# Attention over a cache, one token: V of a head as one load of long runs, its products after both halves of K

## The chip, the cores and the metric

The kernel runs on one core of one Trainium2 chip. The metric is device microseconds of one execution; lower is better.

## The reference

One token (`x` of 512 numbers) goes through two branches that a gate mixes. Branch A is attention of 32 query heads over 8 key/value heads with 32,768 cached rows of 128 numbers each; branch B is a small gated FFN. All tensors are bf16.

```python
def reference(A_x, A_k_cache, A_v_cache, A_wq, A_wo, B_x, B_w_gate, B_w_up, B_w_down, gate_w):
    x = A_x                                               # 1 x 1 x 512
    g = sigmoid((x * gate_w).sum(-1))
    q = (x @ A_wq) as 32 heads of 128                     # wq 512 x 4096
    k, v = each of the 8 cached heads, for 4 query heads  # 8 x 32768 x 128 each
    p = softmax(q @ k.T * 128 ** -0.5)
    a = (p @ v) as 4096 numbers @ A_wo                    # wo 4096 x 512
    b = (silu(x @ B_w_gate) * (x @ B_w_up)) @ B_w_down    # 512 x 1792, 1792 x 512
    return g * a + (1 - g) * b
```

K and V of one cached head are 8.4 MB each, so the eight heads are 134 MB; the five weights add 14 MB. Everything is read once.

## The kernel before

**The stream.** All large loads are issued by SyncE (SP) on one queue, in the order of the list `stream` (lines 67 to 71): wq, K half 0 of head 0, the gate and up weights (`F1`), K half 1 of head 0, the down weights (`F2`); then for each head `g` from 1 on K half 0 of `g`, V half 0 of `g - 1`, K half 1 of `g`, V half 1 of `g - 1`; at the end V of head 7 and wo. A half of K or V is 16,384 rows, 4.194 MB. It is read as 128 runs of 32 KB, one for each partition (lines 294 to 296).

**The slots.** `ring` has five slots of 32 KB a partition. `place` (lines 73 to 78) gives every load its slot: K halves in slots 0 and 2, V halves in 1 and 3, wq in 1, F1 in 4, wo in 2, and the last V half in 0. F2 has a tile of its own, `wd_t`. A load whose slot had another load before it waits in SP until that one is released (`before`, `released`, lines 79 to 83 and 243 to 247): for wq by its products (`sem_pe_q`), for F1 by the FFN's (`sem_pe_h`), for a K half by its scores (`sem_k`, raised by the last group of them), for a V half by its products (`sem_pv`). SP takes its list in order, so a load that waits holds back all behind it. Slot 3 also holds scratch at first: `q_sb`, and the FFN's `sg`, `t1` and `tr`; so the first V half that goes there waits for `sem_tT`, the last step of the FFN's activation (lines 267, 268).

**TensorE.** For each K half, `emit_k` transposes 128 tiles through PSUM in 16 fills (line 404), VectorE copies each fill to SBUF (line 732), and TensorE forms the scores of four fills at a time (line 418). In the middle of it `emit_pt` transposes the probabilities of the head before (line 465), and VectorE copies them to `ET` (line 767). `emit_pv` multiplies a V half by `ET` (line 485). `emit_max` and VectorE form the maximum over both halves (lines 450, 454, 747, 755), and ScalarE then takes the exponentials `P` (line 621). V lags one head: in the pass of head `g` TensorE does K half 0 of `g`, V half 0 of `g - 1`, K half 1, V half 1, the maximum. In the pass of head 0 there is no V yet, and the FFN's products (`emit_ffn`, line 372) take the place of V half 0; they write the PSUM banks `ps_g` and `ps_u`, which are also those of the second half's scores and of the transposed `P`. ScalarE's sigmoid (line 613) and VectorE's `emit_t` (lines 713 to 719) follow it.

**The end.** The last V half comes in two pieces of 2 MB (`sem_ldv`); wo comes in five pieces (`WO_CUT`), each with a semaphore of its own, and its products (line 569) follow the pieces. ScalarE and VectorE write the result row.

Of the kernel before, what the change touches and what calls it, by code (L numbers as in the profile page):

```python
# [5 lines left out]
ACT = mybir.ActivationFunctionType  # L6
# [6 lines left out]
def bass_gated_mix__gqa_block_cached__swiglu_ffn__decode_kernel(  # L13
# [50 lines left out]
    assert NI * PB == 32 and sum(WO_CUT) == WOJ  # L64


    stream = [("wq",), ("K", 0, 0), ("F1",), ("K", 0, 1), ("F2",)]
    for g in range(1, G):
        for hf in range(2):
            stream += [("K", g, hf), ("V", g - 1, hf)]  # L70
    stream += [("V", G - 1, 0), ("V", G - 1, 1), ("wo",)]

    place = {("wq",): 1, ("F1",): 4, ("wo",): 2}
    for g in range(G):
        for hf in range(2):
            place["K", g, hf] = 2 * hf
            place["V", g, hf] = 2 * hf + 1
    place["V", G - 1, 1] = 0
    before = {}
    for i, e in enumerate(stream):  # L80
        for d in stream[:i]:
# [3 lines left out]
    with ExitStack() as es:  # L85
# [8 lines left out]
        sem_ldv = S_("s_ldv")  # L94
        sem_f2 = S_("s_f2")
        sem_ldo = [S_(f"s_ldo{i}") for i in range(len(WO_CUT))]
        sem_x = S_("s_x")
# [132 lines left out]
            "p (k e b d) -> p k e b d", k=HB, e=2, b=2  # L230
        )

        def kv_slot(entry):
            return slot_of(entry).rearrange("p (r d) -> p r d", r=RH)

        wq_v = slot_of(("wq",)).rearrange("p (c n) -> p c n", c=KC)
        f1 = slot_of(("F1",))
# [14 lines left out]
        with nc.Block("main") as block:  # L252
# [8 lines left out]
            @block.sync  # L261
            def _(sp):
                for i, e in enumerate(stream):
                    ld = sem_ld[place[e]] if e in place else sem_f2
                    if e in before:
                        sp.wait_ge(*released[before[e]])
                    elif e == ("V", 0, 1):
                        sp.wait_ge(sem_tT, 1)
                    if e[0] == "wq":
                        sp.dma_start(wq_v, A_wq.rearrange("(p c) n -> p c n", c=KC)).then_inc(  # L270
                            ld, 16
                        )
                    elif e[0] == "F1":
                        sp.dma_start(wg, B_w_gate.rearrange("(p c) f -> p c f", c=KC)).then_inc(
                            ld, 16
                        )
                        sp.dma_start(wu, B_w_up.rearrange("(p c) f -> p c f", c=KC)).then_inc(
                            ld, 16
                        )
                    elif e[0] == "F2":  # L280
                        sp.dma_start(wd, B_w_down.rearrange("(p j) n -> p j n", j=FC)).then_inc(
                            ld, 16
                        )
                    elif e[0] == "wo":
                        src = A_wo.rearrange("(p j) n -> p j n", j=WOJ)
                        j0 = 0
                        for c, n in enumerate(WO_CUT):
                            sp.dma_start(wo_v[:, j0 : j0 + n, :], src[:, j0 : j0 + n, :]).then_inc(  # L288
                                sem_ldo[c], 16
                            )  # L290
                            j0 += n
                    else:
                        kind, g, hf = e
                        src = (A_k_cache if kind == "K" else A_v_cache)[
                            0, g, hf * (S // 2) : (hf + 1) * (S // 2), :
                        ].rearrange("(p r) d -> p r d", r=RH)
                        dst = kv_slot(e)
                        if e == ("V", G - 1, 1):
                            sp.dma_start(dst[:, : RH // 2, :], src[:, : RH // 2, :]).then_inc(
                                ld, 16  # L300
                            )
                            sp.dma_start(dst[:, RH // 2 :, :], src[:, RH // 2 :, :]).then_inc(
                                sem_ldv, 16
                            )
                        else:
                            sp.dma_start(dst, src).then_inc(ld, 16)
                sp.wait_ge(sem_res, 2)
                sp.dma_start(
                    out[0, :, :], row[0:1, :]
                ).then_inc(sem_out, 16)  # L310
                sp.wait_ge(sem_out, 16)

            @block.tensor
            def _(pe):
# [112 lines left out]
                    ins.then_inc(sem_sc, 1)  # L427

                def emit_k(hf):
                    e = ("K", 0, hf)  # L430
                    take(load_sem(e), 16)
                    done = 0
                    for q in range(FPH):
                        emit_fill(kv_slot(e), q)
                        if q + 1 >= NCG * (done + 1) + 2:
                            emit_scores(hf, done)
                            done += 1
                        if q == NCG and hf == 0:
                            emit_o()
                        if q == FPH // 2:  # L440
                            emit_pt(hf)
                    while done < NI:
                        emit_scores(hf, done)
                        done += 1
                    pe.sem_inc(sem_cp, -FPH)
# [23 lines left out]
                        )  # L469
                    ins.then_inc(sem_pt, 1)  # L470

                def emit_pv(hf, halves=False):
                    e = ("V", G - 1 if halves else 0, hf)
                    take(load_sem(e), 16)
                    pe.wait_ge(sem_ptc, hf + 1)
                    src = kv_slot(e).rearrange("p (i c t) d -> p i c t d", i=NI, c=NCG)
                    for i0 in range(0, NI, 2):
                        if i0 > 0 and halves:
                            emit_outb()
                            warm(7)  # L480
                            pe.wait_ge(sem_ldv, 16)
# [12 lines left out]
                    ins.then_inc(sem_pv, 1)  # L494
# [43 lines left out]
                pe.wait_ge(sem_ptc, 1)  # L538
                emit_pt(1)
                emit_o()  # L540
                emit_pv(0)
                pe.wait_ge(sem_em, 1)
                pe.matmul(
                    ps_e[:, 0:H],
# [35 lines left out]
            def _(act):  # L580
# [28 lines left out]
                    ).then_inc(sem_oc, 1)  # L609

                emit_oc(1)
                act.wait_ge(sem_pe_h, 1)
                act.activation(sg[:, :], ps_g, ACT.Sigmoid).then_inc(sem_sg, 1)
                for g in range(G):
                    act.wait_ge(sem_nbias, g + 1)
                    if g < G - 1:
# [1 line left out]
                    for hf in range(2):  # L618
                        f = 2 * g + hf
                        act.wait_ge(sem_pt, f + 1)  # L620
                        act.activation(  # L621
                            P[:, hf, :],
                            ps_sc[hf],
                            ACT.Exp,
                            bias=nbias[:, 0:1],
                            scale=SCALE,
                            accum_out=esum[:, g, hf : hf + 1],
                        ).then_inc(sem_exp, 1)
# [5 lines left out]
            def _(dve):  # L634
# [140 lines left out]
                with dve.Fori(0, G) as it:  # L775
                    for hf in range(2):
# [76 lines left out]
```

## Time and profile before

| what | value |
|---|---|
| time, median of 3 runs | 352.45 us (352.36 to 352.77) |
| the profiled execution's own time | 352.42 us |
| its span in the profile | 350.6 us |
| granted TensorE clock, mean | 0.912 |
| TensorE busy | 259.2 us, 74% |
| VectorE busy | 200.1 us, 57% |
| ScalarE busy | 19.9 us, 6% |
| load queue of SP | 6050 packets, 148.12 MB, 98.5% of 16 engines' span |
| K loads, issue to landing, median of 16 | 25.1 us |
| V loads of 4 MB, issue to landing, median of 15 | 32.8 us |
| wq load, issue to landing | 12.3 us |

The span runs from the first to the last instruction; some 1.8 us of the device time lie around it. Busy shares are of the span. A load's time from issue to landing holds its wait in the queue: SP issues a load as soon as its slot is free, and the DMA engines take the loads in order. In the order of time a row has the start and the duration in us, the engine, the line, the operation, what it writes and reads, the number of instructions merged into the row, and in brackets how long the engine had been idle and what ended that.

### The profile page before, as it was taken

The numbers are of one execution on the slowest core, as the hardware profiler recorded it, in microseconds if no ns is written. First come the engines' busy times: TensorE is split into PE (matmuls) and PEld (weight loads), VectorE is DVE, ScalarE is ACT, GpSimd is POOL, SyncE is SP. The second block draws the span as 40 slices with busy tenths as digits, with TensorE's granted clock in tenths as the row PEclk, the third lists the DMA queues.
The fourth block names the chain that finished last, engine by engine and source line by source line (L and its number), as shares of the span: only waits on it lengthen the run. The fifth ranks groups of instructions, "written<-read, shape, count | busy, mean of one in ns | idle before, by whom it ended". The sixth has DMA issues, their size and how long they took to land. (4 is left out here: it accounts for less than half of the span.)

```text
span 350.6 us, 5679 instructions
## 1 busy us (share of the span) xinstructions
PE 259.2 (74%) x2423; PEld 179.1 (51%) x2423; DVE 200.1 (57%) x368; ACT 19.9 (6%) x57; POOL 1.4 (0%) x8
## 2 busy tenths in 40 slices
PE   0449876989495886858595978858597939777686
PEld 0147153856282846546382847546474718454342
DVE  4148287779284675838283765748265926666210
ACT  1100000300100002000100001000100010000100
POOL 1000000000000000000000000000000000000000
PEclk9999999899989698989789698989769987999899
DMA  8999999999999999999999999999999999999995
GB/s 337 441 402 434 422 440 426 443 441 422 422 437 441 430 422 426 445 441 422 422 434 445 430 422 426 441 441 422 426 422 452 434 422 426 437 445 422 413 419 207
DMA packets 6060, 148.20 MB, mean 423 GB/s; under 512 B 675, under 2 KB 678, under 8 KB 1062
## 3 DMA queue, kind: packets, MB, share of 16 engines
q1 hardware_dynamic: 6050, 148.12, 98.5%
q8 instruction: 4, 0.07, 0.1%
q14 instruction: 2, 0.02, 0.0%
q10 hardware_dynamic: 4, 0.00, 0.0%
HBM read 148.11 MB, written 0.00 MB: 422 GB/s over the span
## 5 line engine op out<-in xcount | busy, mean ns | idle before, releaser
L732 DVE COPY ktT<-ps 128x1024 bf16<-128x1024 bf16 x256 | 163.1, 684 | 81.8 <-PE ps L404 79.2
L404 PE MATMUL ps<-ident_f,ring 128*128 128x128 f32 x1024 | 157.9, 310 | 48.0 <-PEq L317 48.0
L404 PEld LDWEIGHTS ps<-ident_f,ring 128*128 128x128 f32 x1024 | 132.9, 161 | 80.5 <-issue 57.1
L418 PE MATMUL ps<-ktT,qc 128*32 128x512 bf16 x512 | 41.6, 401 | 15.2 <-DVE ktT L732 15.1
L485 PE MATMUL ps<-ring,ET 128*16 128x512 bf16 x512 | 32.0, 393 | 2.8 <-PEq L317 2.1
L485 PEld LDWEIGHTS ps<-ring,ET 128*16 128x16 bf16 x512 | 12.5, 91 | 19.1 <-issue 7.6
L418 PEld LDWEIGHTS ps<-ktT,qc 128*32 128x32 bf16 x512 | 7.9, 95 | 28.0 <-DVE ktT L732 24.2
L737 DVE TENSOR_REDUCE pmaxf<-ps 128x1 f32<-128x512 f32 x16 | 11.1, 691 | 13.8 <-DVEq L736 13.8
L589 ACT ACTIVATE qc<-qz 128x112 bf16<-128x112 bf16 x8 | 2.4, 296 | 197.7 <-DVE gsel L755 194.2
L502 PEld LDWEIGHTS ps<-osel,pv_sb 128*128 128x128 f32 x80 | 11.9, 228 | 1.4 <-DVE pv_sb L773 1.0
L621 ACT ACTIVATE P<-ps,nbias 128x512 bf16<-128x512 f32 x16 | 10.8, 676 | 29.0 <-DVE gsel L755 29.0
L502 PE MATMUL ps<-osel,pv_sb 128*128 128x4 f32 x80 | 11.3, 265 | 0.8 <-DVE pv_sb L773 0.5
L773 DVE COPY pv_sb<-ps 128x512 f32<-128x512 f32 x10 | 6.8, 682 | 6.5 <-PE ps L485 6.5
L465 PE MATMUL ps<-ident,P 128*128 128x128 bf16 x72 | 7.0, 219 | 1.7 <-ACT P L621 1.2
L767 DVE COPY ET<-ps 128x512 bf16<-128x512 bf16 x18 | 7.5, 414 | 1.3 <-PE ps L465 1.3
L372 PE MATMUL ps<-ring,xT 128*1 128x448 bf16 x32 | 6.6, 984 | 0.0
L747 DVE TENSOR_REDUCE gm<-ps 1x4 f32<-1x128 f32 x8 | 2.2, 279 | 7.7 <-DVEq L746 7.7
L465 PEld LDWEIGHTS ps<-ident,P 128*128 128x128 bf16 x72 | 5.4, 98 | 2.1 <-ACT P L621 1.3
L345 PE MATMUL ps<-ring,xT 128*1 128x512 bf16 x32 | 3.6, 626 | 3.6 <-PEq L317 3.6
L454 PE MATMUL ps<-gm,ones_f 1*128 1x4 f32 x16 | 2.8, 243 | 4.6 <-PEq L317 4.6
L326 PE MATMUL ps<-ones_bf,x_row 1*128 1x1 bf16 x4 | 0.3, 173 | 7.9 <-DMA gw_row<-in_gate_w_dram 7.9
L692 DVE CAST ring<-ps 128x512 bf16<-128x512 f32 x2 | 1.3, 685 | 7.5 <-PE ps L345 7.5
(70 smaller groups left out, 50.3 us busy)
## 6 DMA issues: line engine op xcount, KB each, us to landing
ring<-in_A_k_cache_dram SPq DMA_DIRECT2D x16, 4096.0 KB, 25.1
ring<-in_A_v_cache_dram SPq DMA_DIRECT2D x15, 4096.0 KB, 32.8
ring<-in_A_wq_dram SPq DMA_DIRECT2D x1, 4096.0 KB, 12.3
ring<-in_A_v_cache_dram SPq DMA_DIRECT2D x2, 2048.0 KB, 29.4
ring<-in_A_wo_dram SPq DMA_DIRECT2D x1, 2048.0 KB, 22.4
ring<-in_B_w_gate_dram SPq DMA_DIRECT2D x1, 1792.0 KB, 25.3
ring<-in_B_w_up_dram SPq DMA_DIRECT2D x1, 1792.0 KB, 29.2
wd_t<-in_B_w_down_dram SPq DMA_DIRECT2D x1, 1792.0 KB, 43.3
```

The lines of the kernel that those rows point to most:

```text
L345: ins = pe.matmul(ps_q[i][32 * c : 32 * c + 1, :], xT[:, k : k + 1], wq_v[:, k, n0 : n0 + 512], start=(k == 0), stop=(k == KC - 1),)
L372: ins = pe.matmul(acc[32 * c : 32 * c + 1, :], xT[:, k : k + 1], wt[:, k, c * FW : (c + 1) * FW].rearrange("d (i j) -> d j i", j=FC), star ...
L404: ins = pe.transpose(stb[:, t * 64 : (t + 2) * 64], two.bitcast(FP32), ident_f[:, :])
L418: ins = pe.matmul(ps_sc[hf][32 * c : 32 * c + 32, :], qc[:, e, 24 - PB * i : 56 - PB * i], kt[:, e, :], start=(i == 0 and e == 0), stop=(i ...
L465: ins = pe.transpose(ps_pt[:, hf * 512 + m * 128 : hf * 512 + (m + 1) * 128], P[:, hf, m * 128 : (m + 1) * 128], ident[:, :],)
L485: ins = pe.matmul(ps_pv[32 * c : 32 * c + 2 * PB, :], ET[:, hf, col : col + 2 * PB], src[:, i0 : i0 + 2, c, 2 * m : 2 * m + 2, :].rearrang ...
L502: ins = pe.matmul(ps_m[:, M_OT : M_OT + HPG], pv_sb[:, r * DH : (r + 1) * DH], osel[:, r * HPG : (r + 1) * HPG], start=(r == 0), stop=(r = ...
L621: act.activation(P[:, hf, :], ps_sc[hf], ACT.Exp, bias=nbias[:, 0:1], scale=SCALE, accum_out=esum[:, g, hf : hf + 1],).then_inc(sem_exp, 1)
L732: dve.tensor_copy(ktT[:, q % NKT, :], pst[q % NST]).then_inc(sem_cp, 1)
L737: ins = dve.tensor_reduce(pmaxf[:, hf : hf + 1], ps_sc[hf], AX.X, ALU.max)
L767: dve.tensor_copy(ET[:, hf, :], ps_pt[:, hf * 512 : (hf + 1) * 512]).then_inc(sem_ptc, 1)
L773: dve.tensor_copy(pv_sb[:, :], ps_pv).then_inc(sem_pvc, 1)
```

## The change

V of a head becomes one load of 8.4 MB in which each partition gets one run of 64 KB; it fills slots 2 and 3. So that the rows of a partition stay the same ones for K and V, a K half now takes 32 KB out of each 64 KB. K halves are in slots 0 and 1. The stream is K half 0, K half 1, V of the head before. wq has slot 4, F1 has slot 2, and wo takes slot 4, where wq was. The last V goes to slots 0 and 1, where the last K was, as three loads (4 MB, 2 MB, 2 MB), the second after the release of K half 1.

TensorE does both K halves, then the maximum, then both products of V of the head before. In the pass of head 0 the FFN comes after the maximum and waits for both exponentials, since its banks are in use until then. ScalarE's sigmoid of the FFN follows the exponentials of head 0, and VectorE's `emit_t` follows the maximum of head 0. The load of V of head 0 waits for the FFN's products (F1's slot) and for `sem_tT` (the scratch in slot 3). All other arithmetic is the same.

```diff
-    stream = [("wq",), ("K", 0, 0), ("F1",), ("K", 0, 1), ("F2",)]
+    stream = [("wq",), ("K", 0, 0), ("K", 0, 1), ("F1",), ("F2",)]
     for g in range(1, G):
-        for hf in range(2):
-            stream += [("K", g, hf), ("V", g - 1, hf)]
-    stream += [("V", G - 1, 0), ("V", G - 1, 1), ("wo",)]
-
-    place = {("wq",): 1, ("F1",): 4, ("wo",): 2}
+        stream += [("K", g, 0), ("K", g, 1), ("V", g - 1)]
+    stream += [("V", G - 1), ("wo",)]
+    place = {("wq",): 4, ("F1",): 2, ("wo",): 4}
     for g in range(G):
-        for hf in range(2):
-            place["K", g, hf] = 2 * hf
-            place["V", g, hf] = 2 * hf + 1
-    place["V", G - 1, 1] = 0
+        place["K", g, 0] = 0
+        place["K", g, 1] = 1
+        place["V", g] = 2 if g < G - 1 else 0
...
+        def v_slot(s0):
+            return ring[:, s0 : s0 + 2, :].rearrange("p s (r d) -> p (s r) d", r=RH)
...
-                released[("V", g, hf)] = (sem_pv, 2 * g + hf + 3)
+            released[("V", g)] = (sem_pv, 2 * g + 4)
...
-                    elif e == ("V", 0, 1):
+                    if e == ("V", 0):
                         sp.wait_ge(sem_tT, 1)
...
+                    elif e[0] == "K":
+                        src = A_k_cache[0, e[1], :, :].rearrange("(p h r) d -> h p r d", h=2, r=RH)
+                        sp.dma_start(k_slot(e[2]), src[e[2]]).then_inc(ld, 16)
                     else:
...
+                        src = A_v_cache[0, e[1], :, :].rearrange("(p r) d -> p r d", r=2 * RH)
+                        if e[1] < G - 1:
+                            sp.dma_start(v_slot(2), src).then_inc(ld, 16)
+                            continue
+
+                        v = v_slot(0)
+                        r0 = 0
+                        for sem, n in (
+                            (sem_ldv[0], RH),
+                            (sem_ldv[1], RH // 2),
+                            (sem_ldv[2], RH // 2),
+                        ):
+                            if r0 == RH:
+                                sp.wait_ge(*released["K", G - 1, 1])
+                            sp.dma_start(v[:, r0 : r0 + n, :], src[:, r0 : r0 + n, :]).then_inc(
+                                sem, 16
...
                 with pe.Fori(0, G) as g:
                     emit_k(0)
+                    emit_k(1)
+                    emit_max()
                     with pe.If(g > 0):
                         emit_pv(0)
+                        emit_pv(1)
                     with pe.Else():
+                        pe.wait_ge(sem_exp, 4)
+                        pe.wait_ge(sem_ptc, 2)
                         emit_ffn()
                         pe.wait_ge(sem_t1, 2)
-                    emit_k(1)
-                    with pe.If(g > 0):
-                        emit_pv(1)
-                    emit_max()
...
                 emit_oc(1)
-                act.wait_ge(sem_pe_h, 1)
-                act.activation(sg[:, :], ps_g, ACT.Sigmoid).then_inc(sem_sg, 1)
                 for g in range(G):
...
                         ).then_inc(sem_exp, 1)
+                    if g == 0:
+                        act.wait_ge(sem_pe_h, 1)
+                        act.activation(sg[:, :], ps_g, ACT.Sigmoid).then_inc(sem_sg, 1)
                     emit_oc(g + 2)
...
-                        if hf == 0:
-                            with dve.If(it == 0):
-                                emit_t()
+                    with dve.If(it == 0):
+                        emit_t()
```

More of the change, by code (lines that the diff above doesn't have):

```diff
@@ L93, in bass_gated_mix__gqa_block_cached__swiglu_ffn__decode_kernel @@
         sem_ld = [S_(f"s_ld{i}") for i in range(NSLOT)]
-        sem_ldv = S_("s_ldv")
+        sem_ldv = [S_(f"s_ldv{i}") for i in range(3)]
         sem_f2 = S_("s_f2")
@@ L231, in bass_gated_mix__gqa_block_cached__swiglu_ffn__decode_kernel, with k_slot @@
         )
-        def kv_slot(entry):
-            return slot_of(entry).rearrange("p (r d) -> p r d", r=RH)
+        def k_slot(hf):
+            return ring[:, hf, :].rearrange("p (r d) -> p r d", r=RH)
+        def v_slot(s0):
+            return ring[:, s0 : s0 + 2, :].rearrange("p s (r d) -> p (s r) d", r=RH)
         wq_v = slot_of(("wq",)).rearrange("p (c n) -> p c n", c=KC)
@@ L291, in _ @@
                             j0 += n
-                    else:
[L293 to L300, printed above, removed]
-                            )
[L302 to L306, printed above, removed]
+                    elif e[0] == "K":
+                        src = A_k_cache[0, e[1], :, :].rearrange("(p h r) d -> h p r d", h=2, r=RH)
+                        sp.dma_start(k_slot(e[2]), src[e[2]]).then_inc(ld, 16)
+                    else:
+                        src = A_v_cache[0, e[1], :, :].rearrange("(p r) d -> p r d", r=2 * RH)
[13 more added lines that the diff above has]
+                                sem, 16
+                            )
+                            r0 += n
                 sp.wait_ge(sem_res, 2)
@@ L429, in emit_k @@
                 def emit_k(hf):
-                    e = ("K", 0, hf)
-                    take(load_sem(e), 16)
+                    take(load_sem(("K", 0, hf)), 16)
                     done = 0
                     for q in range(FPH):
-                        emit_fill(kv_slot(e), q)
+                        emit_fill(k_slot(hf), q)
                         if q + 1 >= NCG * (done + 1) + 2:
@@ L470, in emit_pt, with emit_pv @@
                     ins.then_inc(sem_pt, 1)
-                def emit_pv(hf, halves=False):
-                    e = ("V", G - 1 if halves else 0, hf)
-                    take(load_sem(e), 16)
+                def emit_pv(hf, halves=None):
+                    if halves is not None:
+                        pe.wait_ge(sem_ldv[hf], 16)
+                    elif hf == 0:
+                        take(load_sem(("V", 0)), 16)
                     pe.wait_ge(sem_ptc, hf + 1)
-                    src = kv_slot(e).rearrange("p (i c t) d -> p i c t d", i=NI, c=NCG)
+                    src = v_slot(0 if halves is not None else 2)[:, hf * RH : (hf + 1) * RH, :].rearrange(
+                        "p (i c t) d -> p i c t d", i=NI, c=NCG
+                    )
                     for i0 in range(0, NI, 2):
@@ L480, in emit_pv @@
                             warm(7)
-                            pe.wait_ge(sem_ldv, 16)
+                            pe.wait_ge(sem_ldv[2], 16)
                         for m in range(NM):
@@ L540, in _ @@
                 emit_o()
-                emit_pv(0)
+                emit_pv(0, halves=False)
                 pe.wait_ge(sem_em, 1)
```

## The prediction

> **What bounds the kernel now.** I read the page first, then the issues of the load queue, then the chain, then the order of time around the first head. On the page, the row of the DMA engines and the table of queues:
>
> ```profile
> DMA  8999999999999999999999999999999999999995
> ...
> q1 hardware_dynamic: 6050, 148.12, 98.5%
> ...
> DMA ring<-in_A_wo_dram 7%; PE ps L404 2%; PE ps L418 1%; SPq L288 0%; DVE ktT L732 0%; DVE row L824 0%; PE ps L569 0%; PE ps L465 0%
> ```
>
> All 38 inner slices have the 16 DMA engines at 9 tenths or more, the one load queue fills 98.5% of the span, and what ends last is the last load, wo. TensorE is busy for 74%, VectorE for 57%. So the kernel is one stream of 148 MB, and its time changes only if the stream stops, or if its bytes move at another rate. The chain's few percent of TensorE ahead of wo is only the release that let wo be issued at 320.8 us; wo then landed 25.6 us later because V stood in the queue ahead of it.
>
> The rate comes from the order of time: TensorE's first fill of a head waits for K half 0 from head 2 on.
>
> ```profile
> 95.44 3.87 PE L404 MATMUL ps<-ident_f,ring 128*128 128x128 f32 x20 [3.66 <-PEq L317]
> ...
> 289.74 4.49 PE L404 MATMUL ps<-ident_f,ring 128*128 128x128 f32 x20 [4.72 <-PEq L317]
> ```
>
> Heads 2 and 7 start 194.30 us apart, 38.86 us a head. A head is four loads of 4.194 MB, so 431.7 GB/s and **9.72 us a slot**. The same view gives the due times of the stream, which I need below: K half 0 of head 2 lands at 95.4, so the load ahead of it ends at 95.4 - 9.7 = 85.7.
>
> The queue never ran dry. Its issues around the first heads, in order of time:
>
> ```profile
> 37.22 0.33 SPq L306 DMA_DIRECT2D ring<-in_A_k_cache_dram  x1
> 37.59 0.43 SPq L306 DMA_DIRECT2D ring<-in_A_v_cache_dram  x1
> 58.16 0.33 SPq L306 DMA_DIRECT2D ring<-in_A_k_cache_dram  x1
> 58.53 0.43 SPq L306 DMA_DIRECT2D ring<-in_A_v_cache_dram  x1
> 75.17 0.33 SPq L306 DMA_DIRECT2D ring<-in_A_k_cache_dram  x1
> ```
>
> At 37.6 two slots are queued behind the FFN weights; the next is asked for at 58.2. K half 0 of head 2, issued at 75.2, lands 20 us later: the stream has some 8 us in hand there, and more elsewhere.
>
> **What the Trainium skill says.** "DMA: Bandwidth & Descriptors", section "Where 436 GB/s comes from": the write ports give 435.2 GB/s in all. The trace agrees with 431.7 as a rate close under it, so long runs can gain 0.8% of it at most. The same page, "Latency and other measured facts": a row pitch of 512 KiB in HBM read at 207 GB/s against 214 in full, and only megabyte pitches halved it. No run here has a pitch over 32 KB. "TensorE: Matmul & The Clock Gate", "Part 1: The HAM clock gate": after an idle window of about 3.4 us the array runs at half rate. The trace agrees: TensorE did little from 58.4 to 61.6 us, and the windows read 0.50 after it. "ScalarE: Activation LUTs", "What ACT_TABLE_LOAD costs": 1283 ns for a change of set; the trace has 1.28 us.
>
> **The change, part by part.**
>
> *Long runs.* V of heads 0 to 6 is 128 packets of 64 KB where it was 256 of 32 KB; the last V keeps 32 KB and 16 KB runs. That removes 7 x 128 = 896 packets, 56 on each of 16 engines. A packet's fixed cost: 32 packets of 32 KB an engine take 38.86 us, 1214 ns each; at 435.2/16 = 27.2 GB/s the bytes alone take 1205, so 9.7 ns at most. The trace's packet records say the same: a 32 KB packet takes 1218 ns and a 16 KB one 615, which leaves 12. Gain 56 x 12 = **0.67 us**; 0 if a run of 64 KB is cut in two.
>
> *Pitch.* A K half now reads 32 KB of every 64 KB, and V starts at each 64 KB. Bytes are the same. I take 0; bounds 0 (nothing here can rise above the port rate) and +1% of the 305 us of K and V, +3 us.
>
> *Order in the steady state.* A head, counted from the landing of its K half 0: half 0 takes TensorE 13.6 us (95.44 to about 109.0), half 1 then 11.9 (77.03 to 88.92), the maximum 2.5 to 3, so it is ready at 28. Half 1 landed at 9.7, V of the head before lands at 29.2, and its products take 2 x 1.9 us warm or 2 x 3.4 cold: done by 36, before K of the next head at 38.9. Releases against the queue: K half 0 freed at 13.3, needed by 29; half 1 freed at 25.3, needed by 39; V freed at 36, needed by 48.6. **Cost nothing**, covered by at least 12 us of queued loads; without that cover each microsecond late would be a microsecond of end. Moving emit_max ahead of the products costs nothing either: it fills the wait for V.
>
> *The tail.* The last V goes to slots 0 and 1, freed by K at about 13 and 25 us of a head and needed at 29 and 39. wo has a slot that has been free since the start. Bytes and pieces after the last K are as before and wo still ends last, so 0. The products of the second half come after the first whole half landed, at 328.5 as before.
>
> *The first head.* Here the order does reach the stream. The FFN now runs after K half 1 and the exponentials (its banks are those of the scores and the transposed P), V of head 0 takes the slot of the gate and up weights, and its load waits for the FFN and for tT. SP is one queue: the loads behind V (both K halves of head 2) wait with it. The lines that time it:
>
> ```profile
> 36.79 0.63 PE L418 MATMUL ps<-ktT,qc 128*32 128x512 bf16 x8 [0.94 <-DVE ktT L732]
> ...
> 37.39 6.64 PE L372 MATMUL ps<-ring,xT 128*1 128x448 bf16 x32
> ...
> 46.02 0.65 DVE L719 STREAM_TRANSPOSE tT<-ring 128x448 bf16<-128x448 bf16 x1
> ```
>
> ```profile
> 57.73 0.63 PE L418 MATMUL ps<-ktT,qc 128*32 128x512 bf16 x8 [0.94 <-DVE ktT L732]
> ...
> 61.44 1.28 ACT L621 ACT_TABLE_LOAD   x1
> ...
> 63.98 0.20 ACT L621 ACTIVATION_READ_ACCUMULATOR P<-ps,nbias 128x1 f32 x1
> ...
> 77.03 3.29 PE L404 MATMUL ps<-ident_f,ring 128*128 128x128 f32 x24
> ```
>
> Half 0 ends at 37.4. Half 1 (landed by then) takes 11.9 and some 0.2 for the reduce of half 0 that now stands in front of VectorE's first copy: 49.5. From the end of half 1 to the second exponential is 64.2 - 58.4 = 5.8: 55.3. The FFN starts at 55.5 and takes 6.64 warm: 62.1. From its end to the end of tT is 46.67 - 44.03 = 2.64: 64.8, and V is issued at **64.9**. TensorE has done little from 49.5 on, so part of the FFN runs at half clock: 0 to 1.7 us more (half of one 3.4 us window); I take 0.9: **65.8**. The sigmoid now lies between two exponentials, so two more table loads: one lies beside the FFN (at line 584 the load ran at 1.54 us, long before its wait ended), the other in head 1, where nobody waits for P before V lands. If the first stands behind the wait, +1.28.
>
> When is V due? In the stream V of head 0 covers the two places that end at 85.7. An empty queue needs the 12.3 us of the wq load from issue to landing, then 9.7 for the second 4 MB: 22.0. So the issue is due at 85.7 - 22.0 = **63.7**. V is 65.8 - 63.7 = **2.1 us late**, and all that follows is as much later. The wq row may hold a slow start of the very first load, so 0.7 less is possible. Packets of instruction fetch each delay one engine by about 1.1 us; some may now fall after the stop: 0 to +1.1.
>
> What is late next: half 0 of head 1 runs from 64.9 to about 78.8, half 1 to 90.7, and the two K loads of head 2 go out at 79 and 91 where 86 and 95 would do. Products of head 0 end by 99 at the latest; V of head 1 is needed by 105. So one stop, not a row of them.
>
> **Sum:** +2.1 - 0.67 = +1.4 us on this execution's own 352.42 (span 350.6 and 1.8 around it), 0.03 under the median shown: **353.8**.
>
> **The rivals.** *No stop* (0.27): a warm FFN, a short exponential chain or a quick start of an idle queue puts V in at its due time. Then only packets count: 352.42 - 0.67 = 351.8, same or just faster. For it: 64.9 warm is only 1.2 us past 63.7, and 0.7 of that may be the first load's own. Against: three of my four open terms make V later. It decides at an issue of 63.7. *A long stop* (0.13): a full window at half clock and the table load in line, 64.9 + 1.7 + 1.3 = 67.9, 4.2 late, 356.0. *The pitch costs* (0.12): 1% gives 353.8 + 3 = 356.9; the port rate, not HBM, binds in the trace, which speaks against it. *The runs are cut* in two packets of 32 KB: then the 0.67 is missing, 354.5; inside the likeliest case (0.48).
>
> **How the numbers follow.** A measurement of this kernel tells about 0.2%, 0.7 us, from no change: faster is under 351.75, slower over 353.15. No stop splits 0.10 faster, 0.17 same; the likeliest case 0.42 slower, 0.06 same; long stop 0.13 slower; pitch 0.11 slower, 0.01 same. That is 0.10, 0.24, 0.66. The likeliest case alone spans 352.9 to 354.9; with the others, 351.6 to 356.9.
>
> **What would show it.** Right: the issue of V of head 0 at 65 to 67 us, one slice near 65 us with a dip in GB/s, K of head 2 starting at 97 to 98, and 38.8 us a head after it. The FFN row over 6.64 us shows the half clock. Wrong: no dip (no stop), a period over 39 us a head (pitch), a second dip in any later slice (a release that I put as early), or packets not down by about 900.

## The result and the profile after

The changed kernel takes 354.04 us (median of 6 runs, 353.54 to 354.38) against 352.36 us for the kernel before beside it (352.22 to 352.77): a ratio of 1.0046, 95% interval 1.0033 to 1.0058. It is **slower by 1.7 us**; 353.8 was predicted. The profiled execution took 354.20 us with a span of 352.4, 1.8 more than the span of before. A ratio leaves out single runs that lie over 1.5% above the fastest of the same kernel; where there were such runs, their times are given.

The page of the changed kernel, its DMA rows and its load queue:

```profile
DMA  8999999898998999999999999989999899899995
GB/s 346 428 417 421 429 438 450 322 476 357 443 502 365 476 409 424 476 409 420 420 417 476 417 417 431 506 372 417 435 458 476 357 454 491 365 476 405 396 423 206
...
q1 hardware_dynamic: 5042, 148.11, 98.0%
```

1008 packets fewer (896 data packets, the rest completion writes of loads that no longer exist), the same bytes, and 98.0% of the span where it was 98.5%. A digit of 8 or a low GB/s alone is no stop: the profile books a packet whole where it starts, and the packets of V are twice as long, so slices swing more. The stop is found with narrow windows. The last three columns are the granted clock of TensorE, the DMA share and GB/s; the first two rows are for the FFN, the others for the stop:

```profile
56.00:57.00 1.00, 1.00 (x8) 0.12 (x4) 0.00 (x0) 0.59 (x1) 0.00 (x0) 0.50 1.14 492
58.00:59.00 1.00, 1.00 (x12) 0.13 (x4) 0.00 (x0) 0.00 (x0) 0.00 (x0) 0.61 0.91 393
...
62.00:63.00 1.00, 0.07 (x4) 0.00 (x0) 0.31 (x1) 0.54 (x1) 0.00 (x0) 1.00 1.06 459
63.00:64.00 1.00, 0.00 (x0) 0.00 (x0) 0.96 (x2) 0.00 (x0) 0.00 (x0) 1.00 0.31 131
64.00:65.00 1.00, 0.00 (x0) 0.00 (x0) 0.67 (x2) 0.00 (x0) 0.00 (x0) 1.00 0.15 66
65.00:66.00 1.00, 0.51 (x3) 0.54 (x4) 0.00 (x0) 0.00 (x0) 0.00 (x0) 0.81 2.45 803
```

From 63 to 65 us hardly a packet starts; then those of V start together. By the packet records an engine was idle for 1.7 us on the mean, and its first packet of V took 2.7 to 3.4 us where 2.42 is usual, another 0.75 us an engine. The cause is in the order of time of the changed kernel, the queue's issues and the FFN that they wait for:

```profile
37.31 12.29 SPq L295 DMA_DIRECT2D ring<-in_A_k_cache_dram  x2
...
55.31 1.28 ACT L641 ACT_TABLE_LOAD   x1
...
55.44 6.64 PE L380 MATMUL ps<-ring,xT 128*1 128x448 bf16 x32 [3.56 <-PEq L325]
...
64.06 0.65 DVE L732 STREAM_TRANSPOSE tT<-ring 128x448 bf16<-128x448 bf16 x1
64.80 0.33 SPq L299 DMA_DIRECT2D ring<-in_A_v_cache_dram  x1
```

In the kernel before the FFN takes the same 6.64 us, from 37.39 us, where the granted clock is 1.00:

```profile
40.00:42.00 2.00, 2.00 (x12) 0.26 (x8) 0.00 (x0) 0.00 (x0) 0.00 (x0) 1.00 1.03 429
```

V of head 0 is issued at 64.80 us, right after tT. A load lands engine by engine. By the trace's landing records the last engine finishes V at 86.75 us; in the kernel before the load in that place finished at 85.59. From there the stream runs without a stop, and faster than before:

```profile
135.32 2.67 PE L412 MATMUL ps<-ident_f,ring 128*128 128x128 f32 x20 [2.75 <-PEq L325]
...
290.44 4.04 PE L412 MATMUL ps<-ident_f,ring 128*128 128x128 f32 x20 [4.46 <-PEq L325]
```

Heads 3 and 7 start 155.12 us apart: 38.78 us a head against 38.86. What the prediction had put at nothing is the end. First the kernel before, then the changed one: the products of the last piece of V, and of the last piece of wo.

```profile
338.29 1.04 PE L485 MATMUL ps<-ring,ET 128*16 128x512 bf16 x16 [0.74 <-DMA ring<-in_A_v_cache_dram]
...
348.21 0.38 PE L569 MATMUL ps<-ring,O 128*1 128x256 bf16 x4 [0.24 <-DMA ring<-in_A_wo_dram]
```

```profile
338.97 1.04 PE L496 MATMUL ps<-ring,ET 128*16 128x512 bf16 x16 [0.83 <-DMA ring<-in_A_v_cache_dram]
...
350.01 0.38 PE L581 MATMUL ps<-ring,O 128*1 128x256 bf16 x4 [0.25 <-DMA ring<-in_A_wo_dram]
```

The changed kernel is only 0.68 us behind at the last V, and 1.80 behind at the last wo: the same 4 MB took 9.92 us before and 11.04 after. So the sum as measured is +1.16 (stop) - 0.48 (long runs) + 1.12 (end) = +1.80 us, the difference of the spans. The middle term is what is left between V of head 0 and the last V; six loads at 0.08 us a head give the same.

These are landings of the last engine. The mean of the 16 engines tells it otherwise: V of head 0 is 2.15 us late (84.20 before, 86.35 after), the last piece of V 1.72, the last piece of wo 1.74. So no further time was lost at the end. The stop cost the mean engine 2.15 us; the last engine showed only 1.16 of it at V, because the engines landed 2.0 us apart before and 0.7 us apart after, and the rest came to light at wo, where one engine had fallen behind again.

### The profile page after: what moved, and what is told of

Read it like the earlier page. It is cut to its first block, busy times and chain, and to the rows that moved or that the text cites. A ratio compares the mean times of both kernels' runs of the same rounds, so it can differ in the third digit from the quotient of the medians.

```text
span 352.4 us, 5661 instructions
## 1 busy us (share of the span) xinstructions
PE 266.1 (76%) x2423; PEld 170.1 (48%) x2423; DVE 197.2 (56%) x368; ACT 22.6 (6%) x59; POOL 1.4 (0%) x8
## 5 line engine op out<-in xcount | busy, mean ns | idle before, releaser
L745 DVE COPY ktT<-ps 128x1024 bf16<-128x1024 bf16 x256 | 160.9, 684 | 77.5 <-PE ps L412 75.3
L412 PE MATMUL ps<-ident_f,ring 128*128 128x128 f32 x1024 | 147.8, 293 | 26.4 <-PEq L325 26.0
L412 PEld LDWEIGHTS ps<-ident_f,ring 128*128 128x128 f32 x1024 | 120.1, 150 | 64.1 <-issue 36.3
L426 PE MATMUL ps<-ktT,qc 128*32 128x512 bf16 x512 | 40.8, 394 | 15.4 <-DVE ktT L745 15.1
L496 PE MATMUL ps<-ring,ET 128*16 128x512 bf16 x512 | 46.2, 536 | 7.2 <-PEq L325 4.1
L496 PEld LDWEIGHTS ps<-ring,ET 128*16 128x16 bf16 x512 | 15.9, 117 | 33.6 <-issue 26.7
L750 DVE TENSOR_REDUCE pmaxf<-ps 128x1 f32<-128x512 f32 x16 | 11.1, 692 | 13.7 <-DVEq L749 13.7
L457 PE MATMUL ps<-ident_f,pmax 128*1 128x128 f32 x8 | 2.3, 290 | 9.6 <-PEq L325 9.6
L619 ACT ACTIVATE oT<-ps 128x4 f32<-128x4 f32 x9 | 1.6, 174 | 94.7 <-PE ps L513 94.7
L461 PE MATMUL ps<-gm,ones_f 1*128 1x4 f32 x16 | 3.8, 307 | 4.6 <-PEq L325 4.6
## 6 DMA issues: line engine op xcount, KB each, us to landing
ring<-in_A_wo_dram SPq DMA_DIRECT2D x1, 2048.0 KB, 28.1
```

The costliest lines, as they stand in the source:

```text
L412: ins = pe.transpose(stb[:, t * 64 : (t + 2) * 64], two.bitcast(FP32), ident_f[:, :])
L426: ins = pe.matmul(ps_sc[hf][32 * c : 32 * c + 32, :], qc[:, e, 24 - PB * i : 56 - PB * i], kt[:, e, :], start=(i == 0 and e == 0), stop=(i ...
L461: pe.matmul(ps_m[:, M_NB : M_NB + HPG], ones_f[0:1, :], gm[:, :], start=True, stop=True,).then_inc(sem_pe_nb, 1)
L496: ins = pe.matmul(ps_pv[32 * c : 32 * c + 2 * PB, :], ET[:, hf, col : col + 2 * PB], src[:, i0 : i0 + 2, c, 2 * m : 2 * m + 2, :].rearrang ...
L745: dve.tensor_copy(ktT[:, q % NKT, :], pst[q % NST]).then_inc(sem_cp, 1)
L750: ins = dve.tensor_reduce(pmaxf[:, hf : hf + 1], ps_sc[hf], AX.X, ALU.max)
```

## The experiments

My theory A: one stop in head 0, a small gain of the long runs, and at the end one fetch of instructions. The trace has four packets of 16 KB on the queue of instructions, three by 66 us and one at about 339; each takes 0.9 to 1.1 us. Theory A takes it that each holds up one of the 16 DMA engines. A load is complete with its slowest engine. In the kernel before, the engines are 0.5 us apart ahead of the first fetch and 2.0 us after the third (at the last piece of V, 336.25 to 338.25), and the last fetch costs nothing. The landings show why: twelve engines finish that piece within 0.51 us of the first one, and only eleven the next load, while the last engine keeps its place; so the fetch fell on an engine that was ahead. A stop lets all engines start again together (338.31 to 338.93 in the changed kernel), and then whichever engine is hit ends last: in the changed kernel 15 engines finish wo by 348.88 us and the sixteenth at 349.97. The rivals were the pitch of 64 KB (B; in the second experiment B stands for a run length that does nothing) and the new slots of the end (C).

**The wait on tT taken away** (scratch in another slot, so the FFN's products alone release V):

```diff
-        sg = ring[:, 3, 0 : 2 * FW].bitcast(FP32)
-        t1 = ring[:, 3, 1024 : 1024 + 2 * FW].bitcast(FP32)
-        tr = ring[:, 3, 2048 : 2048 + FW]
+        sg = ring[:, 4, 0 : 2 * FW].bitcast(FP32)
+        t1 = ring[:, 4, 1024 : 1024 + 2 * FW].bitcast(FP32)
+        tr = ring[:, 4, 2048 : 2048 + FW]
...
-                    if e == ("V", 0):
-                        sp.wait_ge(sem_tT, 1)
```

> The changed kernel with the FFN's scratch (sg, t1, tr) in slot 4, so that V of head 0 waits for the FFN's products alone, not for tT. Theory A (one stop of the stream in head 0, long runs a small gain, and a last instruction fetch that costs in full because the stop has lined the 16 engines up): V of head 0 is issued at 62.2 us, ahead of its due time of 63.7; no dip in the DMA rate near 64; its last landing at 85.0 to 85.7; the period stays at 38.78 us a head; the engines keep their spread of about 2 us and the late fetch costs nothing: 351.9 us, 0.5 under the kernel before. Theory C (the extra 1.1 us after the last V comes from the new end, the slots of the last V and of wo): the stop's 1.2 us go, the end's 1.1 stay: 353.0.

Measured: 354.22 us median of 22 runs, from 351.64 to 357.47; ratio 1.0039 (1.0018 to 1.0060). The issue came at 62.19 as expected, and the fastest runs are those of theory A, but most are not: a miss. In the profiled execution (353.44 us) fourteen engines went on without a gap and two were idle for 1.1 and 1.5 us, yet the engines' first packets of V took up to 3.9 us where 2.42 is usual, some 0.6 us an engine, and V landed at 86.50. The end behaved as A has it: engines apart, 9.9 us from the last V to the last wo. So theory C falls, and "due at 63.7" was too late a time: that was a due time for an empty queue, and 62.19 is 2.0 us ahead of the first landing of the load before. Two things were to be found: how early a load must go out (theory D: 2 to 4 us ahead, or its first packets are slow even without a gap), and what makes runs differ so (theory E, further down).

**V in two loads of 32 KB runs:**

```diff
-                            sp.dma_start(v_slot(2), src).then_inc(ld, 16)
+                            v = v_slot(2)
+                            sp.dma_start(v[:, :RH, :], src[:, :RH, :]).then_inc(ld, 16)
+                            sp.dma_start(v[:, RH:, :], src[:, RH:, :]).then_inc(ld, 16)
...
-                        take(load_sem(("V", 0)), 16)
+                        take(load_sem(("V", 0)), 32)
```

> The changed kernel with V of heads 0 to 6 as two loads of 32 KB runs, issued one after the other; order, pitch and waits as in the change. Theory A: packets back near 6050, the period back at 38.86 us a head, stop and end as in the change: 0.5 us over the change, 354.5. Theory B (the run length does nothing, and the shorter period comes from the engines being in step or from the order): period stays at 38.78, 354.0.

Measured: 354.38 us median of 11 runs, 354.00 to 356.53; ratio 1.0059 (1.0039 to 1.0079). The median is 0.3 us over that of the change, inside the spread of the runs, but the period settles it; heads 3 and 7 of this kernel:

```profile
136.24 2.67 PE L414 MATMUL ps<-ident_f,ring 128*128 128x128 f32 x20 [1.93 <-PEq L327]
...
291.68 2.67 PE L414 MATMUL ps<-ident_f,ring 128*128 128x128 f32 x20 [1.70 <-PEq L327]
```

155.44 / 4 = 38.86 us a head again. The long runs are worth 0.08 us a head, and the packet records account for most of it: 2420 ns for 64 KB against 2 x 1214, so 8 ns for each of 8 packets an engine. The end was not as expected: a second group of slow packets near 95 us left the engines 1.79 us apart at the last piece of V, and the last 4 MB took 9.92 us.

**The pitch alone**, in the kernel before:

```diff
-                            0, g, hf * (S // 2) : (hf + 1) * (S // 2), :
-                        ].rearrange("(p r) d -> p r d", r=RH)
+                            0, g, :, :
+                        ].rearrange("(p h r) d -> h p r d", h=2, r=RH)[hf]
```

> The kernel before with the reading pattern alone changed: each half of K and of V takes 32 KB out of every 64 KB; loads, order and slots as before. Theory A (pitch costs nothing): 352.4 us, 38.86 us a head within 0.03. Theory B (pitch costs, and the long runs gain more than 12 ns a packet to hide it in the change): a period over 38.95, 353 us or more.

Measured: 352.39 us; ratio 0.9999 (0.9988 to 1.0010), 38.86 us a head. Theory B falls: reading 32 KB out of every 64 KB costs nothing.

**A stop in the kernel before:**

```diff
-                    elif e == ("V", 0, 1):
+                    if e == ("K", 1, 1):
+                        sp.wait_ge(sem_pe_o, 2)
+                    if e == ("V", 0, 1):
```

> The kernel before with one wait added: K half 1 of head 1 waits for the fold of head 1 (sem_pe_o at 2, about 66.4 us) and is issued there, not at 58.2. Theory A: the queue runs dry at about 64; the load lands at 66.5 + 12.3 = 78.8 and not at 75.9, 2.9 us late; from there on the engines are in step, the last V piece is 2.9 late, and the late instruction fetch costs about 1.1 more: 352.4 + 4.0 = 356.4. Theory C (the end of the change, not the fetch, costs the 1.1): 355.3, the delay the same at the last V and at the last piece of wo.

Measured: four runs from 355.77 to 357.91 us, ratio 1.0107 (1.0066 to 1.0147); two more took 363.62 and 363.79, which is not explained. The profiled execution took 355.91 us with a span of 354.1, 3.5 over that of before. The held load was issued at 66.19 and landed at 78.29, 2.4 late; the last V piece was 2.3 late (340.59 against 338.25 by the landing records), the last piece of wo 3.5:

```profile
341.19 1.23 PE L487 MATMUL ps<-ring,ET 128*16 128x512 bf16 x10
...
351.73 0.38 PE L571 MATMUL ps<-ring,O 128*1 128x256 bf16 x4 [0.25 <-DMA ring<-in_A_wo_dram]
```

With the old order, slots and end, a stop alone brings the extra 1.1 us at wo. That supports the fetch: the extra comes with the stop, whatever the end looks like. The trace also answers the rival that the shorter period of the change comes from engines in step: here they are in step too (0.44 us apart at the last piece of V), and a head takes 38.85 us with runs of 32 KB.

**The FFN back at its old place**, after K half 0 of head 0:

```diff
-    stream = [("wq",), ("K", 0, 0), ("K", 0, 1), ("F1",), ("F2",)]
+    stream = [("wq",), ("K", 0, 0), ("F1",), ("K", 0, 1), ("F2",)]
...
                     emit_k(0)
+                    with pe.If(g == 0):
+                        emit_ffn()
+                        pe.wait_ge(sem_t1, 2)
                     emit_k(1)
                     emit_max()
                     with pe.If(g > 0):
                         emit_pv(0)
                         emit_pv(1)
-                    with pe.Else():
...
```

> The changed kernel with the FFN put back to its old place, after K half 0 of head 0 (F1 ahead of K half 1 in the stream; sigmoid and emit_t back too). Long runs, both K halves ahead of V, slots and end stay. Theory D (a load must be issued more than some 2 to 4 us ahead of the queue's end, or the engines' first packets of it are slow): V of head 0 goes out at about 58 us, K half 1 of head 2 at 87, each with 5 us or more in hand; no slow packets after the first load; 38.78 us a head; 351.9 us, within 0.3, with runs as close together as those of the kernel before. Rival (the new order in the steady state or the end costs something by itself): 352.4 or more, or runs that spread over microseconds as those of the moved scratch did.

Measured: 357.25 us, six runs from 356.82 to 360.42; ratio 1.0153 (1.0125 to 1.0181): a miss. The expectation had looked at V alone. With the FFN first, K half 1 of head 0 is released at 58 us, and in the new stream the load that waits for it stands one place earlier, right behind K half 0 of head 1, which ends near 54.5. The row holds that load and the one before it, from 36.28 to the end of the second issue at 58.43:

```profile
36.28 22.15 SPq L295 DMA_DIRECT2D ring<-in_A_k_cache_dram  x2
58.54 0.36 SPq L299 DMA_DIRECT2D ring<-in_A_v_cache_dram  x1
```

The stop moved to another load and grew: that load landed at 71.42 where 66.20 is its time in the changed kernel. The FFN's late place is what the two K halves in a row need.

**A short lead**, in the kernel before (K half 1 of head 1 held until `nbias`, the maximum that the exponentials of head 0 need):

```diff
-                    elif e == ("V", 0, 1):
+                    if e == ("K", 1, 1):
+                        sp.wait_ge(sem_nbias, 1)
+                    if e == ("V", 0, 1):
```

> The kernel before with K half 1 of head 1 held until the first nbias (about 61.1 us), so that it is issued some 3 us ahead of the queue's end at 64.2, not 6. Theory D (short lead costs): no gap, but first packets of this load of 1.3 to 2.5 us where 1.21 is usual, 0.2 to 0.7 us an engine, and runs from 352.4 to 355. Rival (only an empty queue costs): 352.4, no slow packets, no spread.

Measured: 352.41 us median of 22 runs, 15 of them within 0.5 of the kernel before, the others up to 356.82; ratio 1.0017 (1.0003 to 1.0031). The profiled one is of the others (354.13): TensorE was late (K half 0 released at 39.0 us, not 37.2), the issue came at 64.34, all but three engines had run dry, and the first packets took 1.5 to 2.2 us. So in most runs the hold cost nothing, and the one slow run with a trace was a real stop. What a lead of 3 us costs, that trace can't tell; all traces together do, at the end of this section.

**A longer stop** in the changed kernel (V of head 0 waits for the fold of head 1 too, the small products that gather a head's output, as in the stop above):

```diff
                     if e == ("V", 0):
                         sp.wait_ge(sem_tT, 1)
+                        sp.wait_ge(sem_pe_o, 2)
```

> The changed kernel with V of head 0 held until the fold of head 1 as well (sem_pe_o at 2, about 70.3 us where it was 64.8). Theory A (past the due time each microsecond of issue is one of end): 5.5 us more than the change, 359.5; V of head 0 lands at 92.3. Rival (the queue has slack that takes part of it up later): under 358.

Measured: 360.20 us, four runs from 359.40 to 360.37; ratio 1.0215 (1.0201 to 1.0230). V was issued at 71.09, 6.29 us after the issue in the changed kernel, and the span is 358.4, 6.0 longer. Theory A holds: past the due time the end moves by nearly the whole delay.

**The change again**, beside these:

> The changed kernel as it is, beside the others on one chip: 354.0 within 0.4; V of head 0 issued at 64.8, slow first packets after it, 38.78 us a head.

Measured: three runs at 354.0 to 354.3 and three at 357.2 to 357.6; ratio 1.0087 (1.0053 to 1.0121). The profiled one (span 355.4) shows where the 3 us come from. Its first K half, and the same row in the first profile of the change:

```profile
28.74 1.09 PE L412 MATMUL ps<-ident_f,ring 128*128 128x128 f32 x4
...
30.74 2.82 PE L412 MATMUL ps<-ident_f,ring 128*128 128x128 f32 x12
```

```profile
28.39 0.63 PE L412 MATMUL ps<-ident_f,ring 128*128 128x128 f32 x4
...
29.52 1.53 PE L412 MATMUL ps<-ident_f,ring 128*128 128x128 f32 x12
```

The same 12 transposes take 2.82 us or 1.53: TensorE ran at about half rate for longer. The trace's first record of the full clock comes at 35.1 us here and at 28.1 us in the first profile. (The clock column reads 1.00 there in both; it has no record before the first change of the clock, so the durations decide.) The release of K half 0, and then V, follow:

```profile
40.54 12.29 SPq L295 DMA_DIRECT2D ring<-in_A_k_cache_dram  x2
68.06 0.33 SPq L299 DMA_DIRECT2D ring<-in_A_v_cache_dram  x1
```

Both issues are 3.2 to 3.3 us later than in the first profile, and the span is 3.0 longer. In the four traces of the kernel before and of its variants K half 0 is released between 36.3 and 39.0 us, but there the load that depends on it has 6 us in hand (58.2 against the queue's end at 64.2).

**The first K half warm** (nine idle matmuls ahead of it):

```diff
                 emit_q()
+                for _ in range(9):
+                    pe.matmul(
+                        ps_w,
+                        ident[:, 0:1],
+                        ident[:, :].unsqueeze(1).to_broadcast([128, 4, 128]),
+                        start=True,
+                        stop=True,
+                    )
```

> The changed kernel with nine idle matmuls of 512 columns between the q products and K half 0 of head 0, where TensorE has nothing to do; they add no result. Theory E (what moves the issue of V of head 0 from 64.8 to 68.1 between runs is how long TensorE is at half clock in K half 0 of head 0, after its idle time): K half 0 is released at about 35 us where it was 37.3 to 40.5, V of head 0 goes out at 62 to 63, 352 to 353, and no runs near 357. Rival (the half clock does not follow from the idle time there): as the change, with runs at 354 and at 357.

Measured: 353.78 us, 12 of 14 runs between 352.6 and 354.2, one at 351.93 and one at 356.75; ratio 1.0038 (1.0022 to 1.0054). The mechanism is as expected: the first 20 transposes took 2.67 us where they had taken 4.50, K half 0 was released at 35.5, V went out at 63.03, and the group at 357 is down to one run. The gain did not come: V landed at 87.64. The faster engines had just run dry, the slower ones had not (0.4 us idle on the mean), so the engines were not lined up, and on top of that first packets were slow on most of them, by 0.7 us an engine on the mean. The mean engine finished V at 85.20, 1.15 earlier than in the first profile of the change, but two engines came 2.1 and 2.8 us after the median. This time the last 4 MB took 9.92 us.

**The FFN later still**, in the pass of head 1 after the products, F1 behind wq in slot 4, scratch behind F1; and the same **with the nine idle matmuls**:

```diff
-    place = {("wq",): 4, ("F1",): 2, ("wo",): 4}
+    place = {("wq",): 4, ("F1",): 4, ("wo",): 4}
...
-                    if e == ("V", 0):
-                        sp.wait_ge(sem_tT, 1)
...
-                    with pe.Else():
+                    with pe.If(g == 1):
                         pe.wait_ge(sem_exp, 4)
...
-                    with dve.If(it == 0):
+                    with dve.If(it == 1):
```

> The changed kernel with the FFN put into the pass of head 1, after the products of V of head 0; F1 follows wq in slot 4 and the FFN's scratch lies behind it, so V of head 0 waits for nothing. Theory A (the loss is only the late issue of V of head 0): V of head 0 is issued right after K half 1 of head 1, at 50 to 53 us with 10 us in hand; no slow packets after the first load; 38.78 us a head; 351.9 us, 0.5 under the kernel before, a little more where K half 0 of head 0 runs throttled and K half 1 of head 1 goes out at 53. Rival (the new order costs something in the steady state or at the end): 352.5 or more without any stop in the stream.

> The FFN in the pass of head 1 and the nine idle matmuls together. Theories A and E: every load of the first heads has 4 us or more in hand; 351.8 to 351.9, with runs no wider apart than 0.5, faster than the kernel before by 0.15%. Rival: 352.4, the gain of the long runs is eaten elsewhere.

Measured: 351.75 us alone and 351.85 with the matmuls; ratios 0.9982 (0.9975 to 0.9990) and 0.9982 (0.9975 to 0.9989), 15 runs from 351.62 to 352.49 and 18 from 351.62 to 352.00, so the matmuls add nothing once the leads are long. **Both beat both kernels**, by 0.6 to 0.7 us against the one before. With the matmuls the page has the queue full again, and the issues show the leads:

```profile
q1 hardware_dynamic: 5042, 148.11, 98.5%
```

```profile
36.47 12.30 SPq L294 DMA_DIRECT2D ring<-in_A_k_cache_dram  x2
48.82 0.43 SPq L298 DMA_DIRECT2D ring<-in_A_v_cache_dram  x1
70.38 12.28 SPq L294 DMA_DIRECT2D ring<-in_A_k_cache_dram  x2
```

V of head 0 goes out at 48.8, some 15 us ahead of the queue's end. The steady state and the end of the change are kept, so neither costs anything by itself; what the change lost began with the stop in head 0.

**The end in all 13 traces.** Each has a fetch of instructions between 337 and 346 us, within or just ahead of the last 4 MB. Where the engines were 1.79 us or more apart at the last piece of V (eight traces), the last 4 MB took 9.91 to 9.97 us. Where they were 1.18 us or less apart (five: the change twice, the stop and the short lead in the kernel before, the longer stop), they took 10.4 to 11.1. The mean engine took 10.05 to 10.08 in all 13. So one late engine makes the difference, and the spread of the engines decides whether it shows.

**The lead in all 13 traces.** Call lead the time from a load's issue to the first landing of the load ahead of it, and a packet slow when it takes over 1.1 times the usual time of its size. Four loads had a lead of 1.1 to 2.1 us: each has 13 to 21 slow packets at its start. The seven whose queue had run dry on most engines have 15 or 16. Four with 2.6 to 3.1 us have three or four each. With 3.3 us or more no load has more than two. So theory D holds, with its limit near 3 us.

## Why the prediction was right, point by point

- *The bound.* Right: one stream; the end moved only with stops, packets and the slowest engine. (The 25.6 us to the landing of wo are those of its last pieces from their own issue; from the first issue at 320.8 us to the last landing at 348.17 it is 27.4. Nothing rests on it.)
- *The steady state, the tail's order and the pitch at nothing.* Right: no later stop, 38.78 us a head, and the pitch alone gave a ratio of 0.9999. The Trainium skill's row on pitch (from "DMA: Bandwidth & Descriptors", "Latency and other measured facts") starts at 512 KiB; here 64 KB cost nothing. One line of it was short: the products of head 0 ended at 100.4, not by 99, still 5 us ahead of the queue's end at 105.5, where the load that waits for them has to follow.
- *Long runs, -0.67.* Right in kind, too large: 0.48 between V of head 0 and the last V, for six of the seven loads. The fixed cost of a packet is 8 ns by the 64 KB record and 10 by the period, not the 12 taken from 16 and 32 KB; the prediction's own bound of 9.7 would have given 0.54.
- *The stop, +2.1.* The chain was right to 0.1 us: the issue at 64.9 for a warm FFN, measured 64.80; the table load hidden beside the FFN, at 55.31. (The page cited for it, "ScalarE: Activation LUTs" of the Trainium skill, has 1283 ns for the load alone and 2.66 us with a drain; in the trace of before the exponential starts 0.01 us after the load's 1.28, so the load alone was the right price.) The term that failed is the 0.9 for the half clock: the clock read 0.50 in the window 56 to 57 us and the FFN took 6.64 us all the same. With 64.80 the rule "22.0 from issue to landing" gives 86.8, measured 86.75: a loss of 1.16 for the last engine.
- *The due time of 63.7.* Good for a load that is already late; as a threshold it failed. Issues at 62.2 and 63.0 still lost about 1 and 2 us at V's landing; a load has to be issued some 3 us ahead of the queue's end, here by about 61 us, an estimate from the leads of all traces and the first landing at 64.1.
- *The instruction fetch, 0 to +1.1.* Named and then taken at 0; it was 1.12. The two mis-sized terms, +0.9 too much and 1.1 too little, cancelled, and that was luck: the forecast of 353.8 was right partly by it. Counted by the mean engine it is the same luck in other terms. V was then due at 62.65 us (84.20 less the 21.55 from issue to mean landing), 1 us ahead of the 63.7 worked out for the last engine, and the 0.9 that was too much for the clock made up for it: 2.1 predicted, 2.15 lost.
- *The signs.* Packets, the dip and 38.8 us a head came as named. The issue at 64.80 was just ahead of the 65 to 67 us named. K half 0 of head 2 landed at 96.41, but its first fill started at 100.28 and not at 97 to 98, since TensorE had the products of head 0 until then.
- *What I did not see.* I took the end of K half 0 at 37.4 us as fixed. K loads that wait for it went out between 36.3 and 40.5 us in these runs (35.5 with the idle matmuls), and since the change has nothing in hand behind it, the spread goes to the end: three of the six runs of the change beside the later experiments took 357 us, outside the forecast's 351.6 to 356.9. The long stop among the rivals had about the size (356.0), not the cause.

**Open:** why the first packets after an empty or nearly empty queue are slow (1.5 to 2.2 us for 32 KB where 1.21 is usual) was not separated from address or descriptor work; the limit near 3 us is read from loads that happened to have those leads, not from one load moved step by step. The records don't name the engine of a fetch, and no run took the late fetch away: that it is what delays the one engine rests on its time and on the landings of the 13 traces. That the matmuls ahead of the first K half remove the runs at 357 rests on 14 runs with one of them left.

## What to carry to other kernels

In a kernel bound by one load queue, list for each load when it can be issued and when the queue ahead of it ends; the smallest difference is the kernel's margin, and it must exceed the 3 us of lead that a load needed here and what the start of the work that frees its slot varies by, here some 4 us. A reordering that keeps all bytes can still spend that margin, and moving the late work to cure one load can starve the one before it; work that nobody needs until the end, like this FFN, belongs behind the loads that it would hold. Compare the landings of the mean engine too, not the last one's alone: a stop can hide part of its cost until a later delay brings it out. Judge a gain of 0.1% by the period of the loop in the trace, which repeats here within 0.02 us from head to head, before judging it by run times.

## What the runs showed of the hardware

- The FFN's 32 strided matmuls took 6.64 us at a granted clock of 0.50 in their first 3 us and 6.64 us in the kernel before at 1.00: the clock did not set their pace.
- A stop costs more than its idle time. In the change the engines were idle for 1.7 us on the mean, and their first packets cost another 0.75 us an engine (0.6 to 0.8 in the traces with a stop or a short lead). It also lines the engines up (2.0 us apart before, 0.7 after), and a later delay of one engine that the spread had hidden then shows, here 1.1 us.
- A load issued just ahead of the queue's end pays much like one on an empty queue: in the 13 traces 13 to 21 slow first packets at a lead of 1.1 to 2.1 us, three or four at 2.6 to 3.1, at most two from 3.3 on. With V issued at 63.0 us the last engine even landed later (87.64) than with V issued at 64.8 (86.75), though the mean engine was done at 85.20 against 86.35.
- A packet of 64 KB took 2420 ns, two of 32 KB 2 x 1214: with V in long runs a head took 38.78 us, with short runs 38.85 or 38.86.
